# The first expert block's first half and the lists that lead to it, moved ahead of parts of attention unit 10

## The chip, the cores and the metric

The kernel runs on one core of a Trainium2 chip. A time is the device time of one execution in microseconds (us). The core's engines work side by side, each through its own list of instructions in order: TensorE (PE, with its weight loads shown apart as PEld), VectorE (DVE), ScalarE (ACT), GpSimd (POOL) and SyncE (SP), which here issues transfers. An instruction waits for semaphores that others raise, and what stands behind it on its engine waits with it.

## The reference

Attention with random features, then a mixture of eight experts of which each row takes one:

```
proj = einsum('bhsd,md->bhsm', x, omega)             # x: q or k, scaled; 8 batches, 8 heads, 576 rows
phi = exp(h - max(h)) / sqrt(m),  h = proj - sum(x*x)/2
kv = einsum('bhsm,bhsd->bhmd', phi(k), v);  z = sum(phi(k))
attn = (phi(q) @ kv) / (phi(q) . z + 1e-6)           # x of the experts: (4608, 512)
e_idx = argmax(x @ w_gate);  gate_w = softmax(...)[e_idx];  eom = sigmoid(x @ w_output_gate)
out[mask] = gate_w * eom * (relu(x[mask] @ w1[e]) @ w2[e])     # mask: rows with e_idx == e
```

## The kernel before

Rows are cut into four chunks of two batches (1152 rows, nine tiles of 128). A **unit** u is one head of one chunk, 8 per chunk and 32 in all; 128 columns hold its keys' and its queries' features. When a chunk's eight units are done, its rows are sorted into **items**: up to 128 rows of one expert, whose indices are lists that a gather follows. Items run as expert blocks while the next chunks' units go on. So units 8 to 15 run beside the first items.

Every step has a short name; a table `ORDER` (line 70 on) lists all of them, some 3200, in one order, and each engine runs its own steps in that order. A second string, `BANKS`, gives the PSUM bank to each step that opens one, and `FILL` the number of filler products in each of six places. A filler is a product of two constants (512 columns) whose result nobody reads. The names that matter here, for unit u, item n and third g of a unit's nine tiles:

- `ld.t.u`, `ld.v.u`: loads of a unit's turned keys and queries and of its values (SP). `hi.u`, `lo.u`: their fp16 halves, `xhi` on ACT (L588) and `xlo` on POOL (L591).
- `pp.u.g`: projection (PE, L681). `mx.2u.g`, `mx.2u+1.g`: maxima of keys and of queries (DVE, L699). `nb.u.g`: the bias from them (DVE). `ex.2u.g`, `ex.2u+1.g`: exponentials (ACT, L716); they free the bank of `pp`.
- `kv.u`: keys times values (PE, L804); `kvh.u`, `kvs.u`: its halves (ACT, DVE); `kt.u`: these sums turned (PE, L840); `ke.u` (ACT, L849) and `kg.u` (PE, L846): their product with the gates' weights; `gh.u`, `gl.u`: its halves.
- `eh`, `el`, `eT.u`: the queries' halves (ACT, POOL L739) and their transposition by a transfer (SP, L781). `pn.u.0`, `pn.u.5`: numerators of five and four tiles (PE, L867); `xf`: the division (DVE).
- `assign.0`, `places.0`, `lists.0` (DVE), `pid.0` (PE, L1306), `gi.0` (DVE, L1313 and L1339), `controls.0` (DVE): the first chunk's lists of row indices and control words.
- `gx.n`: the gather of an item's rows (POOL, L1584); `<9` ties it behind `eT.9`. `xt.n`: their transposition (SP, L1595).
- `w0h.1.i`, `w0l.1.i`: the halves of the first expert's first weights, which are loaded ahead on the guess that the first item is expert 1's (ACT and DVE, L521 and L526). `sw.0.1`: a branch on ACT and DVE that makes these halves anew if the guess is wrong; it is passed by here.
- `hA.n`, `hB.n`: the two halves of an expert block's first product (PE, L1618); `relu.n`, `rest.n`: halves of its result; `out.n`: the second product (L1651).
- `warm.i`: `FILL[i]` filler products (PE, L479).

`hA.n` waits for `xt.n`, for its bank, and on ACT and DVE for the end of `sw.n.1`, which counts as a writer of the weights' halves whether or not it is passed by:

```
add((name, n), "PE", ..., after=[("xt", n), *cuts_of(n, 1, halves_of[g])] ...
plan.add(("sw", n, w), ("ACT", "DVE"), lambda w=w: switch(w),
         after=[flag_step[n, 1, ("ACT", "DVE")], ("bring", n, w)] + last)
```

Of the kernel before, what the change touches and what calls it, by code (L numbers as in the profile page):

```python
# [113 lines left out]
bounded.0 eh.21 gl.9 xf.8.0 mx.22.0 advance.0:0 ld.t.13 xf.8.5:0 pp.11.1 flag.0.1.ACT+DVE mx.23.0 w0h.2.3 advance.0:1 mx.22.1 pn.9.5 xf.9.5:0 w0h.2.2
advance.0:2 gx.2<9 xt.0 mx.23.1 nb.11.0:0 kv.10.0 el.21 xf.8.5:1 nb.11.1:0 advance.0:3 xf.9.5:1 nb.11.0 w0h.1.3 nb.11.1 advance.0:4 kv.10.1 ex.22.1
ld.t.14 xf.8.5 eT.10 kvh.10 advance.0:5 xf.9.5 w0l.1.3 pn.9.0 kvs.10 xf.9.0:0 w0l.1.2 flag.0.1.SP ex.23.0 pp.11.2 ex.23.1 xf.9.0:1 bring.0.1 ex.22.0
kt.10 advance.0:6 sw.0.1 hi.13.0 pp.12.0 xf.9.0 bring.1.1 advance.0:7 mx.24.0 w0h.2.1 advance.0:8 lo.13.0 warm.3 hA.0 mx.22.2 ke.10 sqr.12 w0h.2.0
mx.25.0 mx.23.2 relu.0.0 advance.0:9 nb.12.0:0 nb.11.2:0 kg.10 advance.0:10 nb.12.0 nb.11.2 ld.v.12 lga.8 w0l.2.1 gx.1<9 hB.0 gh.10 gl.10 rest.0.0
ex.22.2 ex.23.2 w0l.2.2 w0l.2.3 sqa.13 relu.0.1 kv.11.0 ex.24.0 pp.12.1 advance.0 kv.11.1 pp.12.2 w0l.2.0 bring.0.2 sw.0.2 eh.23 mx.24.1 out.0.0
ex.25.0 sw.1.1 el.23 mx.24.2 ld.t.15 xh.8 mx.25.1 nb.12.1:0 ld.n.15 hi.14.0 bring.2.1 kvh.11 pn.10.5 nb.12.1 mx.25.2 ld.n.14 vh.12 ld.v.13 xt.1 eT.11  # L120
rest.0.1 bring.1.2 nb.12.2:0 xl.8 ex.25.1 xf.10.5:0 ex.24.1 nb.12.2 sqr.13 vl.12 out.0.1 pn.10.0 ex.24.2 ex.25.2 xf.10.5:1 sqa.14 xf.10.5 pp.13.0
eh.24 os.0 lo.14.0 kvs.11 sw.1.2 mx.26.0 hA.1 eh.25 kt.11 mx.27.0 ke.11 pp.13.1 ld.v.14 xf.10.0:0 xf.10.0:1 nb.13.0:0 relu.1.0 hB.1 el.24 sqr.14
xf.10.0 kg.11 nb.13.0 xh.9 mx.26.1 ex.26.0 rest.1.0 ld.n.16 mx.27.1 kv.12.0 nb.13.1:0 el.25 nb.13.1 ex.27.0 sw.2.1 sqa.15 pp.13.2 ld.t.16 mx.26.2
ex.27.1 mx.27.2 nb.13.2:0 out.1.0 gh.11 xt.2 eT.12 ex.26.1 relu.1.1 vh.13 gl.11 nb.13.2 pp.14.0 ld.n.17 bring.2.2 ex.27.2 rest.1.1 ex.26.2 sqr.15
mx.28.0 kv.12.1 sqa.16 kvh.12 eh.26 mx.29.0 hi.15.0 lga.9 kvs.12 pn.11.0 pp.14.1 mx.28.1 out.1.1 nb.14.0:0 eh.27 nb.14.0 gx.3<11 xl.9 vl.13 mx.29.1
nb.14.1:0 ex.28.0 put.0<11 bring.3.1 kt.12 el.26 xf.11.0:0 os.1 hA.2 xh.10 rows.4 sqr.16 ex.29.0 nb.14.1 pn.11.5 ex.29.1 xt.3 pp.14.2 ex.28.1 kv.13.0
xf.11.5:0 sw.2.2 ke.12 mx.28.2 lga.10 xf.11.0:1 xf.11.5:1 kg.12 hi.16.0 hB.2 xf.11.5 mx.29.2 gh.12 sw.3.1 nb.14.2:0 gl.12 lo.15.0 nb.14.2 relu.2.0
ld.v.15 ex.28.2 ld.n.18 pn.12.5 ex.29.2 rest.2.0 kv.13.1 relu.2.1 ld.t.17 vh.14 kvh.13 pn.12.0 pp.15.0 el.27 eh.28 kvs.13 eT.13 kt.13 sqa.17 vh.15
xl.10 hA.3 xf.12.5:0 gx.4<12 mx.30.0 ke.13 mx.31.0 kg.13 vl.14 xf.11.0 sqr.17 gh.13 xf.12.0:0 xf.12.0:1 xf.12.5:1 gl.13 xh.11 eh.29 xf.12.0 out.2.0
# [1660 lines left out]
```

## Time and profile before

| | |
|---|---|
| median of 3 runs | 623.45 us (618.49, 623.45, 624.92) |
| the profiled execution | 623.36 us, its span 621.6 us |
| busy in the span | PE 587.6, PEld 451.1, DVE 408.0, ACT 413.9, POOL 361.2 us |
| granted PE clock, mean | 0.996 |

The profiled execution's time is 1.8 us longer than its span, which runs from its first to its last instruction. PE is the engine with the most work; over the span it idles 34 us, and where it does, another engine or a transfer is late.

### The profile page before, as it was taken

Reading aid. Unit: us, or ns where it says so; the run is one execution under the profiler, and the core shown is the slowest. Engines: PE = TensorE matmul, PEld = TensorE weight load, DVE = VectorE, ACT = ScalarE, POOL = GpSimd, SP = SyncE. Lnnn points to the kernel's source line nnn. Section 1 sums busy time; section 2 is a strip of 40 time slices with the busy share of each in tenths; the row PEclk is TensorE's granted clock in tenths of the full one; section 3 lists DMA queues with packets and bytes.
Section 4 is the critical chain, followed back from the end, with each engine's and each line's share of the span. In section 5 each row is a group of like instructions: output and inputs, shape, how many; then the busy total and the mean of one; then the engine's idle time right before and its main releaser. Section 6 shows DMA issues by size and latency. Waiting matters only on the chain. (4 is left out here: it accounts for less than half of the span.)

```text
span 621.6 us, 21399 instructions
## 1 busy us (share of the span) xinstructions
PE 587.6 (95%) x8442; PEld 451.1 (73%) x8442; DVE 408.0 (66%) x1114; ACT 413.9 (67%) x971; POOL 361.2 (58%) x265
## 2 busy tenths in 40 slices
...
GB/s 296 274 291 293 314 269 195 246 268 246 346 208 247 213 215 263 194 197 245 285 236 247 145 203 204 150 227 221 184 147 338 93 91 132 295 65 91 109 289 33
DMA packets 144686, 133.74 MB, mean 215 GB/s; under 512 B 104606, under 2 KB 124448, under 8 KB 143264
## 3 DMA queue, kind: packets, MB, share of 16 engines
...
## 5 line engine op out<-in xcount | busy, mean ns | idle before, releaser
L716 ACT ACTIVATE ef<-pp,nb 128x128 f32<-128x128 f32 x576 | 164.6, 393 | 40.2 <-DVE nb L710 29.6
L699 DVE TENSOR_REDUCE pp<-pp 128x3 f32<-128x384 f32 x192 | 106.7, 562 | 46.6 <-PE pp L681 40.6
L739 POOL TENSOR_TENSOR es<-ef,es 128x1152 f16<-128x1152 f32 x44 | 104.5, 2378 | 38.4 <-ACT es L737 21.7
L1618 PE MATMUL ph<-xt,w1h 128*128 128x128 f16 (+1 forms) x2048 | 122.2, 217 | 1.0 <-issue 0.6
L1618 PEld LDWEIGHTS <-w1h 128*128 128x128 f16 x2048 | 113.5, 98 | 6.9 <-issue 1.7
L1584 POOL DMA_INDIRECT gx<-rows,gi x38 | 41.0, 1079 | 130.1 <-ACTq L1551 63.3
L1629 DVE SCALAR_TENSOR_TENSOR hl<-ph,hh 128x512 f16<-128x512 f32 (+1 forms) x76 | 50.6, 666 | 99.7 <-ACTq L1551 73.8
L1651 PEld LDWEIGHTS <-hh 128*128 128x128 f16 x560 | 51.5, 98 | 54.5 <-issue 0.8
L1625 ACT ACTIVATE hh<-ph 128x512 f16<-128x512 f32 (+1 forms) x76 | 44.7, 591 | 65.6 <-PE ph L1618 50.9
L1618 PE MATMUL ph<-xt,w1l 128*128 128x128 f16 (+1 forms) x1024 | 66.7, 218 | 2.3 <-issue 2.3
L591 POOL TENSOR_TENSOR xlo<-xt,xhi 128x1152 f16<-128x1152 f32 x24 | 57.2, 2381 | 11.2 <-ACT xhi L588 11.1
L1651 PE MATMUL po<-w2h,hh 128*128 128x512 f16 x240 | 62.6, 383 | 0.0
L1651 PE MATMUL po<-w2h,hl 128*128 128x512 f16 x240 | 62.3, 382 | 0.0
L1651 PE MATMUL po<-w2l,hh 128*128 128x512 f16 x240 | 61.6, 379 | 0.0
L1694 ACT ACTIVATE os<-po,gx 128x512 f32<-128x512 f32 (+1 forms) x35 | 24.2, 692 | 54.9 <-PE po L1651 45.6
L1618 PEld LDWEIGHTS <-w1l 128*128 128x128 f16 x1024 | 58.5, 98 | 2.8 <-issue 2.8
L737 ACT CAST es<-ef 128x1152 f16<-128x1152 f32 x44 | 51.6, 1178 | 4.4 <-DMA et<-es 3.5
L1651 PEld LDWEIGHTS <-hl 128*128 128x128 f16 x280 | 27.5, 99 | 33.9 <-issue 1.1
L907 POOL TENSOR_TENSOR xs<-xf,xs 128x576 f16<-128x576 f32 x32 | 40.9, 1281 | 17.4 <-DVE nb L710 6.6
L867 PE MATMUL pn<-kvs,et 128*128 128x81 f16 x768 | 39.9, 201 | 3.1 <-DMA et<-es 1.2
L867 PEld LDWEIGHTS <-et 128*128 128x128 f16 x768 | 34.3, 97 | 8.7 <-issue 3.1
L681 PEld LDWEIGHTS <-xhi 64*128 64x128 f16 x864 | 25.6, 94 | 15.7 <-issue 9.0
(210 smaller groups left out, 1047.9 us busy)
## 6 DMA issues: line engine op xcount, KB each, us to landing
...
xn<-kqn SPq DMA_DIRECT2D x31, 576.0 KB
xt<-kqt SPq DMA_DIRECT2D x31, 576.0 KB
rawv<-v SPq DMA_DIRECT2D x32, 325.0 KB
rows<-xs SPq DMA_DIRECT2D x16, 576.0 KB
...
```

The lines of the kernel that those rows point to most:

```text
L591: plan.add(("lo", u, x), ("POOL",), lambda t0=t0, t1=t1: nc.gpsimd.tensor_tensor(out=xl(u)[:, t0:t1], in0=xt32(u)[:, t0:t1], in1=xh(u)[:, ...
L699: nc.vector.tensor_reduce(out=spare(g, 0)[:, i], in_=banks["pp", 2 * u + i, g][:, 0:3, :], op=ALU.min, axis=AX.X)
L716: nc.scalar.activation(ef(2 * u + i)[:, c, :], banks["pp", 2 * u + i, g][:, c % 3, :], AF.Exp, bias=nb(u)[:, i, c : c + 1], scale=-SK)
L737: nc.scalar.copy(es(slot_es(n))[:, 0], ef(n))
L739: nc.gpsimd.tensor_tensor(out=es(slot_es(n))[:, 1], in0=ef(n), in1=es(slot_es(n))[:, 0], op=ALU.subtract)
L867: nc.tensor.matmul(pn[:, c - c0, :], a[:, c, :], w[:, :, 0 if c < 4 else 1], start=(i == 0 and c == c0), stop=(c == NC - 1 and i == len(op ...
L907: nc.gpsimd.tensor_tensor(out=x[:, :, P + o : P + o + D], in0=xf(u)[:, :, 0:D], in1=x[:, :, o : o + D], op=ALU.subtract)
L1584: return nc.gpsimd.indirect_dma_start(out=gx(n), out_offset=None, in_=rows[0 : (j + 1) * NC * P], in_offset=bass.IndirectOffsetOnAxis(ap=t ...
L1618: nc.tensor.matmul(ph[:, f4, 0:w_], w[qd][:, kk, fo : fo + P], xt(n)[:, x, 0:w_], start=(z == 0 and f4 == 0 and x == 0), stop=(z == 1 and ...
L1625: nc.scalar.activation(hh(n)[:, sl, 0:w_], banks["ph", n, g][:, :, 0:w_], AF.Relu)
L1629: nc.vector.scalar_tensor_tensor(out=hl(n)[:, sl, 0:w_], in0=banks["ph", n, g][:, :, 0:w_], scalar=0.0, in1=hh(n)[:, sl, 0:w_], op0=ALU.ma ...
L1651: nc.tensor.matmul(po, x(n)[:, f, :], w[f // 2][:, f % 2, :], start=(f == 0 and a == 0), stop=(f == FC - 1 and a == 2))
```

## The change

Only the three tables change; every step and its computation stay, but for four filler products.

```
@@ ORDER, around unit 10 (two lines of each kernel)
-assign.0:3 places.0:1 warm.1 kg.8 pp.10.2 assign.0:4 hi.12.0 ex.21.0 kvs.9 lo.11.0 assign.0:5 kt.9 mx.20.2 gh.8 assign.0:6 w0h.1.2 places.0 assign.0
-eT.9 mx.21.2 controls.0:0 lists.0:0 ke.9 nb.10.2:0 gl.8 controls.0:1 lists.0:1 controls.0:2 warm.2 pn.8.0 nb.10.2 sqa.12 lists.0 warm.5 pid.0 w0l.1.1
...
+assign.0:3 places.0:1 warm.1 kg.8 pp.10.2 assign.0:4 hi.12.0 ex.21.0 kvs.9 lo.11.0 assign.0:5 kt.9 gh.8 assign.0:6 w0h.1.2 places.0 assign.0 eT.9
+lists.0:0 ke.9 lists.0:1 warm.2 sqa.12 lists.0 pid.0 mx.20.2 gi.0:0 gi.0 gx.0<9 lo.12.0 mx.21.2 nb.10.2:0 gl.8 pn.8.0 warm.5 controls.0:0 nb.10.2
...
-FILL = (5, 6, 8, 4, 4, 3,)
+FILL = (5, 6, 7, 1, 4, 3,)
```

The moves, in full: `lists.0`, `pid.0`, `gi.0` and `gx.0` go ahead of `mx.21.2`, `nb.10.2`, `gl.8`, `pn.8.0`, `controls.0` and `w0l.1.1`, and `lists.0` ahead of `mx.20.2` too; `lo.12.0` goes behind `gx.0`. `ld.v.11` and `ld.t.13` go behind `xt.0`. `w0h.1.3` goes ahead of `w0h.2.3` and `w0h.2.2`; `ex.22.0` goes ahead of `ex.22.1`, `ex.21.1` ahead of `ex.21.2`. `sw.0.1` and `hA.0` go ahead of `kt.10` and `pp.12.0`. `warm.3` goes from the place right ahead of `hA.0` to one between `kv.10` and `pn.9.0`, and has one product in place of four; `warm.2` has seven in place of eight. `BANKS` follows: the filler left in `warm.3` takes the bank that `ex.22.0` leaves, and `hA.0` takes it after that. From `hB.0` on the two orders are the same.

On DVE the difference at the lists reads as follows; `pp_2` is the bank of unit 10's last third, `rt`, `r_eq`, `r_itc`, `pid` and `gi` are the lists':

```order
-L699 TENSOR_REDUCE pp_2_1802<-pp_2_1802 128x3
 L1157 COPY r_exs<-rt_1605 128x9
 L1079 TENSOR_TENSOR place<-cmt,rt_1605 128x1152
 L1160 TENSOR_TENSOR rt_1605<-rt_1605,cft 128x8
+L1172 COPY rt_1605<-cft 128x18
+L1175 TENSOR_TENSOR r_eq<-keys,rt_1605 128x9x8
+L1183 TENSOR_TENSOR r_itc<-r_eq,rt_1605 128x18x8
+L699 TENSOR_REDUCE pp_2_1802<-pp_2_1802 128x3
+L1313 TENSOR_REDUCE pid_1860<-pid_1860 128x8
+L1339 CAST gi_1872<-pid_1860 128x8
 L699 TENSOR_REDUCE pp_2_1802<-pp_2_1803 128x3
```

The first maximum now stands between the lists and their cast to indices, and the second behind that cast.

On SP, around the first gather's transposition, before (`et_1842` is `eT.9`, `rawv_1962` `ld.v.11`, `xt_1978` `ld.t.13`, `xt_2044` `xt.0`) and then now (`xt_2040` is `xt.0`, `rawv_2042` `ld.v.11`, and `xt_2044` is `ld.t.13`):

```order
L781 DMA_TRANSPOSE et_1842<-es_1749 128x18x128
L660 DMA rawv_1952<-v 128x650
L660 DMA rawv_1962<-v 128x650
L658 DMA xt_1978<-kqt 128x1152
L1595 DMA_TRANSPOSE xt_2044<-gx_1968 128x8x128
L658 DMA xt_2073<-kqt 128x1152
```

```order
L781 DMA_TRANSPOSE et_1841<-es_1749 128x18x128
L660 DMA rawv_1955<-v 128x650
L1595 DMA_TRANSPOSE xt_2040<-gx_1874 128x8x128
L660 DMA rawv_2042<-v 128x650
L658 DMA xt_2044<-kqt 128x1152
L658 DMA xt_2075<-kqt 128x1152
```

The transposition, which waits for the gather, went ahead of two loads.

On PE, from the end of `pp.11.2` (`pp_2_2127`) to the start of `hA.0` (`ph_0`), before and then now; `kv_2049<-cmt` is `kt.10`, `pp_0` is `pp.12.0`, `fill` is `warm.3`:

```order
L681 MATMUL pp_2_2127<-omh,xlo_1830 128x128
L840 LDWEIGHTS kvs_2078
L840 MATMUL kv_2049<-cmt,kvs_2078 128x128
...
L681 LDWEIGHTS xhi_1823
L681 MATMUL pp_0_2179<-omh,xhi_1823 128x128
...
L479 MATMUL fill_2219<-omh 128x512
L1618 LDWEIGHTS w1h_85
L1618 MATMUL ph_0_2224<-xt_2044,w1h_85 128x128
```

```order
L681 MATMUL pp_2_2131<-omh,xlo_1830 128x128
...
L1618 LDWEIGHTS w1h_85
L1618 MATMUL ph_0_2175<-xt_2040,w1h_85 128x128
...
L840 LDWEIGHTS kvs_2080
L840 MATMUL kv_2049<-cmt,kvs_2080 128x128
...
L681 LDWEIGHTS xhi_1823
L681 MATMUL pp_0_2229<-omh,xhi_1823 128x128
```

`hA.0` now follows `pp.11.2` directly, and what stood between them follows `hA.0`; the fillers between them are gone. The steps ahead of `sw.0.1` on ACT are the same ones in both kernels; `ex.22.0`, which stood last of them, is now the first exponential of unit 11.

## Rows read from the trace of the kernel before

**Rows 1.** Page, busy time, share of the span and instructions of each engine

```profile
PE 587.6 (95%) x8442; PEld 451.1 (73%) x8442; DVE 408.0 (66%) x1114; ACT 413.9 (67%) x971; POOL 361.2 (58%) x265
```

**Rows 2.** Stretches: length, busy PE, PEld, DVE, ACT, POOL, clock, DMA share, GB/s

```profile
96.00:112.00 16.00, 13.92 (x209) 10.22 (x208) 15.64 (x57) 15.80 (x39) 9.25 (x6) 1.00 1.02 210
104.00:112.00 8.00, 6.97 (x106) 5.74 (x105) 7.86 (x29) 7.80 (x20) 4.16 (x3) 1.00 1.07 186
112.00:144.00 32.00, 32.00 (x484) 24.67 (x482) 27.27 (x65) 29.97 (x69) 22.62 (x17) 1.00 1.04 262
```

**Rows 3.** Timeline of PE (start us, us, engine line op tiles, idle before)

```profile
106.24 0.61 PE L867 MATMUL pn<-kvs,et 128*128 128x81 f16 x12 [0.26 <-DVE xf L885]
...
107.37 0.33 PE L681 MATMUL pp<-omh,xlo 64*128 64x128 f16 x6
...
108.30 0.27 PE L840 MATMUL kv<-cmt,kvs 128*128 128x128 f16 x2 [0.60 <-DVE den L881]
...
108.91 0.36 PE L681 MATMUL pp<-omh,xlo 64*128 64x128 f16 x6
...
109.39 1.02 PE L479 MATMUL fill<-omh 128*128 128x512 f16 x4
...
110.47 1.95 PE L1618 MATMUL ph<-xt,w1h 128*128 128x128 f16 x32
...
113.23 1.95 PE L1618 MATMUL ph<-xt,w1h 128*128 128x128 f16 x32
```

**Rows 4.** A stretch for line 479 alone, the fillers: length, busy PE, PEld, clock

```profile
95.50:112.00 16.50, 3.73 (x15) 1.33 (x15) 1.00 1.01 206
```

**Rows 5.** Timeline of DVE

```profile
95.64 0.56 DVE L699 TENSOR_REDUCE pp<-pp 128x3 f32<-128x384 f32 x1
...
99.18 1.23 DVE L526 SCALAR_TENSOR_TENSOR w1l<-r,w1h 128x1024 f16<-128x1024 f32 x1
...
100.78 0.15 DVE L1339 CAST gi<-pid 128x8 uint32<-128x8 f32 x1
...
108.22 1.21 DVE L526 SCALAR_TENSOR_TENSOR w1l<-r,w1h 128x1024 f16<-128x1024 f32 x1
```

**Rows 6.** Timeline of POOL

```profile
96.75 2.37 POOL L591 TENSOR_TENSOR xlo<-xt,xhi 128x1152 f16<-128x1152 f32 x1 [0.50 <-ACT xhi L588]
...
101.23 2.03 POOL L1584 DMA_INDIRECT gx<-rows,gi  x1 [2.10 <-DVE den L883]
```

**Rows 7.** Timeline of SP's queue

```profile
94.63 3.23 SPq L781 DMA_TRANSPOSE et<-es  x1
...
99.05 0.38 SPq L658 DMA_DIRECT2D xt<-kqt  x1
...
105.60 1.26 SPq L1595 DMA_TRANSPOSE xt<-gx  x1
```

**Rows 8.** Timeline of ACT

```profile
105.86 0.99 ACT L716 ACTIVATE ef<-pp,nb 128x128 f32<-128x128 f32 x3
...
106.77 2.57 ACT L716 ACTIVATE ef<-pp,nb 128x128 f32<-128x128 f32 x9
...
109.54 1.15 ACT L588 CAST xhi<-xt 128x1152 f16<-128x1152 f32 x1 [0.20 <-ACTq L1546]
...
111.56 0.35 ACT L849 CAST kvf<-kv 128x256 f16<-128x256 f32 x1
```

**Rows 9.** Page, transfers by line, with their size

```profile
xt<-kqt SPq DMA_DIRECT2D x31, 576.0 KB
rawv<-v SPq DMA_DIRECT2D x32, 325.0 KB
```

**Rows 10.** Timeline of PE at two later waits, and a stretch around the second

```profile
350.04 0.32 PE L681 MATMUL pp<-omh,xhi 64*128 64x128 f16 x5 [1.45 <-ACT ef L716]
...
479.18 0.80 PE L1618 MATMUL ph<-xt,w1l 128*128 128x128 f16 x8 [1.06 <-issue]
...
478.00:482.80 4.80, 3.73 (x19) 1.79 (x17) 1.32 (x4) 2.27 (x3) 0.33 (x1) 0.65 0.99 288
```

More of the change, by code (lines that the diff above doesn't have):

```diff
@@ L110 @@
 kt.8 weigh.0:1 nb.10.0 assign.0:0 nb.10.1:0 weigh.0:2 w0h.1.1 ex.20.0 assign.0:1 kvh.9 weigh.0 nb.10.1 assign.0:2 ke.8 ex.20.1 places.0:0 scales.0
-assign.0:3 places.0:1 warm.1 kg.8 pp.10.2 assign.0:4 hi.12.0 ex.21.0 kvs.9 lo.11.0 assign.0:5 kt.9 mx.20.2 gh.8 assign.0:6 w0h.1.2 places.0 assign.0
-eT.9 mx.21.2 controls.0:0 lists.0:0 ke.9 nb.10.2:0 gl.8 controls.0:1 lists.0:1 controls.0:2 warm.2 pn.8.0 nb.10.2 sqa.12 lists.0 warm.5 pid.0 w0l.1.1
-pn.8.5 kg.9 ex.21.2 ex.21.1 gi.0:0 pp.11.0 lo.12.0 controls.0:3 ld.v.10 xf.8.0:0 gi.0 ex.20.2 ld.v.11 controls.0 xf.8.0:1 w0l.1.0 gh.9 gx.0<9
@@ L114 @@
[L114 to L129, printed above, removed]
@@ L130 @@
-bring.4.1 xf.12.5 rest.2.1 pp.15.1 nb.15.0:0 lo.16.0 el.28 sqa.18 kv.14.0 mx.30.1 bring.3.2 vl.15 out.2.1 nb.15.0 xt.4 mx.31.1 ex.30.0 nb.15.1:0
-sw.3.2 xl.11 el.29 bring.4.2 sqr.18 pn.13.0 nb.15.1 ex.31.0 ex.31.1 relu.3.0 rest.3.0 ld.v.16 put.1<12 pp.15.2 lga.11 ld.n.19 kv.14.1 xh.12 hi.17.0
-mx.30.2 hB.3 mx.31.2 xf.13.0:0 nb.15.2:0 nb.15.2 xf.13.0:1 kvh.14 eT.14 xl.12 ex.30.1 kvs.14 ex.31.2 xf.13.0 relu.3.1 pn.13.5 xf.13.5:0 lga.12
+assign.0:3 places.0:1 warm.1 kg.8 pp.10.2 assign.0:4 hi.12.0 ex.21.0 kvs.9 lo.11.0 assign.0:5 kt.9 gh.8 assign.0:6 w0h.1.2 places.0 assign.0 eT.9
@@ new lines @@
+lists.0:0 ke.9 lists.0:1 warm.2 sqa.12 lists.0 pid.0 mx.20.2 gi.0:0 gi.0 gx.0<9 lo.12.0 mx.21.2 nb.10.2:0 gl.8 pn.8.0 warm.5 controls.0:0 nb.10.2
+controls.0:1 controls.0:2 controls.0:3 w0l.1.1 pn.8.5 kg.9 ex.21.1 ex.21.2 pp.11.0 ld.v.10 xf.8.0:0 ex.20.2 controls.0 xf.8.0:1 w0l.1.0 gh.9 bounded.0
+eh.21 gl.9 xf.8.0 mx.22.0 advance.0:0 xf.8.5:0 pp.11.1 flag.0.1.ACT+DVE mx.23.0 w0h.1.3 w0h.2.3 advance.0:1 mx.22.1 pn.9.5 xf.9.5:0 w0h.2.2
+advance.0:2 gx.2<9 xt.0 ld.v.11 ld.t.13 mx.23.1 nb.11.0:0 kv.10.0 el.21 xf.8.5:1 nb.11.1:0 advance.0:3 xf.9.5:1 nb.11.0 nb.11.1 advance.0:4 kv.10.1
@@ new lines @@
+ex.22.0 ex.22.1 ld.t.14 xf.8.5 eT.10 kvh.10 advance.0:5 xf.9.5 w0l.1.3 warm.3 pn.9.0 kvs.10 xf.9.0:0 w0l.1.2 flag.0.1.SP ex.23.0 pp.11.2 ex.23.1
+xf.9.0:1 bring.0.1 sw.0.1 hA.0 kt.10 advance.0:6 hi.13.0 pp.12.0 xf.9.0 bring.1.1 advance.0:7 mx.24.0 w0h.2.1 advance.0:8 lo.13.0 mx.22.2 ke.10 sqr.12
+w0h.2.0 mx.25.0 mx.23.2 relu.0.0 advance.0:9 nb.12.0:0 nb.11.2:0 kg.10 advance.0:10 nb.12.0 nb.11.2 ld.v.12 lga.8 w0l.2.1 gx.1<9 hB.0 gh.10 gl.10
+rest.0.0 ex.22.2 ex.23.2 w0l.2.2 w0l.2.3 sqa.13 relu.0.1 kv.11.0 ex.24.0 pp.12.1 advance.0 kv.11.1 pp.12.2 w0l.2.0 bring.0.2 sw.0.2 eh.23 mx.24.1
```

15 lines of the change are left out of this document (14 added, 1 removed).

## The prediction

> **What bounds the kernel now.** I read the page's busy times first, then equal stretches, then the engines' timelines around the change. TensorE (PE) is busy 95% of the span [rows 1]: whatever delays PE delays the end, and whatever only delays another engine does so when PE runs out of work. The stretches show two states [rows 2]. From 96 to 112 us PE is busy 13.92 of 16 us, while VectorE (DVE) has 15.64 and ScalarE (ACT) 15.80: here those two set the pace and PE waits for them. From 112 to 144 us PE has 32.00 of 32: it is the bound, and a delay or gain it enters with is carried on. So the question is when PE gets into that full stretch. I take as mark the start of hB.0, the second half of the first expert block, at 113.23 [rows 3]: everything from there on stands in the same order in both kernels.
>
> A ceiling comes out of the same rows. Between 96 and 112 us PE idles 16 - 13.92 = 2.08 us, and 3.73 us of its busy time are filler products [rows 2, 4]. If the change removed all of that, it would bring 5.8 us, 0.93% of 623.36 us, the profiled execution's time. So no saving here can pass 1%, which is about what a measurement of this kernel can tell from no change.
>
> **The lists.** On DVE the two maxima of unit 10's last third (0.56 us each, in a stream about 0.46) and w0l.1.1 (1.2 us) stood ahead of the list's cast gi.0; now one maximum stands between lists and gi.0, and that one covers PE's sum pid.0. gi.0 ended at 100.78 + 0.15 = 100.93 [rows 5]. Ahead of it go 0.46 + 1.2 and, of the two maxima, what pid.0 does not take up anyway, about 0.4: some 2.1 us, so it ends near 98.8. Nothing is saved on DVE by that: the same instructions run ahead of w0l.1.2 in both orders, DVE is full, and the list's links now follow each other at once and can stall 0 to 0.3 us.
>
> **The gather and the two queues it is moved past.** gx.0 began at 101.23, 0.3 us behind gi.0 [rows 6]. It is also tied to eT.9, the transposition, whose entry on SP's queue ends at 94.63 + 3.23 = 97.86 and whose data must land later, at the latest at 101.1, since at 101.23 the wait was put down to DVE [rows 6, 7]. So the gather starts between 98.9 and 101.1; I take 100, the middle, a gain of 1.2 us. On GpSimd lo.12.0, which ran from 96.75, now waits behind it, until the gather's 2.03 us are over near 102 [rows 6]; its 2.37 us then end near 104.4, and its only reader in this stretch, pp.12.0, ran at 108.5. That costs nothing.
>
> SP issued the transposition xt.0 at 105.60, 4.37 us behind the gather's start [rows 6, 7]; the same distance gives 104.4 (103.3 to 105.5). xt.0 was not what hA.0 waited for last, so this gains nothing by itself. But ld.v.11 and ld.t.13, the latter issued at 99.05, now stand behind the wait for the gather: with xt.0's 1.26 us and ld.v.11's issue ld.t.13 comes at about 106.2. It feeds hi.13.0, which ACT reached at 109.54 [rows 8]. The two loads hold 325 and 576 KB [rows 9], 0.92 MB; at the 186 GB/s that the stretch from 104 to 112 us moved [rows 2] that is an estimate of 4.9 us from 105.7, so ld.t.13 lands near 110.6 (109.5 to 111.7). ACT then waits 1.1 us (0 to 2.2) at hi.13.0, and relu.0.0 and ke.10 stand behind it. In the trace hi.13.0's start to ke.10's end took 111.91 - 109.54 = 2.37 us [rows 8], so ke.10 ends at 113.0 (111.9 to 114.1). kg.10, one step ahead of hB.0 on PE, waits for ke.10.
>
> **PE.** Two edits meet here. The fillers: warm.2 has one product less and warm.3 three less, four at 1.02 / 4 = 0.25 us each [rows 3]. Those of warm.2 stand where PE waits anyway. Those of warm.3 stood right ahead of hA.0 and ended at 110.41; hA.0 began at 110.47. What hA.0 can start from otherwise: its bank is the one that ex.22.0 leaves, ACT's exponentials end at 106.77 + 2.57 = 109.34, and ACT is past sw.0.1, the branch on the first weights, at 109.54 [rows 8]; DVE's w0l.1.2 ends at 108.22 + 1.21 = 109.43 [rows 5]. So without the fillers hA.0 could have begun near 109.6. These gates do not move: the same exponentials, only in another order, and the same halves of weights stand ahead of sw.0.1 on both engines, and both are full. I take 109.8 for the stalls above (109.6 to 110.1).
>
> The order: kt.10 and pp.12.0, from 108.30 to 108.91 + 0.36 = 109.27 [rows 3], lay in PE's wait and cost nothing. Now they stand behind hA.0, in PE's full stretch, and cost their length: 0.97 us with the pipeline's end, about 0.85 in a stream. What PE has in their place is idle time: pp.11.2 ended at 107.70 [rows 3]. It will end later, since the one filler left now stands ahead of pn.9.0 in the bank that ex.22.0 has to leave, and ex.22.0 is now ACT's first of that unit, at about 105.9 to 106.7: pn.9.0 goes from 106.24 to about 106.9. That is inside the wait too, if hA.0 really starts at 109.8.
>
> **The sum.** hA.0 to the start of hB.0 took 113.23 - 110.47 = 2.76 us, kg.10 among it. Now 109.8 + 2.76 + 0.85 = 113.41, against 113.23: +0.2 us. kg.10 would be free at about 113.1 (112.0 to 114.2) and reached at 113.33, so ke.10 mostly hides behind pp.12.0; for its upper half I add 0.1. Forecast: +0.3 us, 623.36 + 0.3 = 623.7 us. Bounds: with hA.0 at 109.6 and 0.8 for the two it is 0.0; with ke.10 at 114.1 it is 114.3 - 113.23 = +1.1. The profiled execution lies 0.1 us below the median of the three runs, 623.45, which scatter from 618.49 to 624.92; that scatter is larger than any term here.
>
> **Rivals.** *Faster: hA.0 follows pp.11.2 at once.* That is what the smaller fillers look made for. If ACT and DVE came to sw.0.1 some 2 us earlier, hB.0 would start at 107.7 + 2.76 + 0.85 = 111.3, 1.9 us earlier: 621.4. For it speaks that PE idles 2.08 us here; against it that ACT is busy 15.80 of 16 us and nothing is taken off it ahead of the branch.
>
> *Slower: PE's clock falls in the new wait.* Between pp.11.2 and hA.0 PE now stands still for 1.5 to 2 us without fillers, after another 0.7 ahead of the one filler. In this trace the granted clock fell once in the middle of the work: PE idled 1.06 us until 479.18, and the clock averages 0.65 from 478 to 482.8 [rows 10]. That is 4.8 x 0.35 = 1.7 us of PE's work lost, at 1.2 in place of 2.4 GHz for 3.4 us. Against it: at 350.04 an idle time of 1.45 us had no such end, and the clock stayed at 1.00 from 96 to 112 us [rows 2, 10]. It decides from the point at which hA.0 starts at the lower level: 623.7 + 1.7 = 625.4. The Trainium skill bears on it: "TensorE: Matmul & The Clock Gate", Part 1, says that half rate is the default and only recent activity holds the full rate, so fillers that are taken out of a wait are no pure gain. By that rule the time would be this rival's; the fall at 479 agrees with it, the stretch at 350 shows that one gap does not always do it.
>
> *Slower: ld.t.13 comes later than estimated.* Each microsecond beyond 111.7 goes to hi.13.0, ke.10 and kg.10 in full; two more give 623.7 + 0.8 + 2 = 626.5.
>
> *The change does not do what it says.* If eT.9 lands at 101, the gather starts as before and xt.0 lands as before or later; PE's part stays as summed, with hA.0 at 110.1 or so: +0.5, 623.9, hard to tell from the forecast.
>
> **How the numbers follow.** Forecast and the case in which the gather stays, 0.62; the clock 0.20; the faster case 0.10; the late load 0.08. The likeliest gives 623.7. The range goes down to the faster case less the scatter of the runs, 621.4 - 2, and up to the late load's 626.5: 619.5 to 626.5. None of these cases leaves the band of 1% (617.2 to 629.6), so what I give to both sides is what I have not seen in the 480 us behind this stretch, where a shifted start meets branches and transfers anew: 0.05 faster, 0.07 slower, 0.88 the same.
>
> **What would show it.** In the profile after: gx.0 on GpSimd near 100 with lo.12.0 behind it; pn.9.0 near 106.9 behind one filler; idle time on PE of over 1 us ahead of hA.0, ended by ACT, with hA.0 at 109.6 to 110.1; kt.10 and pp.12.0 behind it and hB.0 at 113.2 to 114.3; hi.13.0 at 110 to 111.7, held by a transfer. I am wrong in the mechanism if hA.0 starts ahead of 109.0 (ACT was freer than it looks), if PE's clock reads below 1.00 between 106 and 116 us, or if hB.0 lies outside 113.0 to 114.5; and in the result if the two kernels differ by more than 3 us while hB.0 does not, since the difference then arises behind the change.

## The result, and the profile after

The changed kernel took 629.6 us, median of six runs (625.81 to 634.28), against 622.34 for the kernel before (six runs, 618.49 to 625.94): ratio 1.0123, 95% interval 1.0078 to 1.0168. It is 1.2% slower, outside the range of the prediction. The profiled execution took 632.93 us, its span 631.1.

The page's busy line [rows 1] and the stretches [rows 2] of the changed kernel:

```profile
PE 588.8 (93%) x8438; PEld 453.6 (72%) x8438; DVE 411.8 (65%) x1114; ACT 414.6 (66%) x971; POOL 362.4 (57%) x265
```

```profile
96.00:112.00 16.00, 10.41 (x131) 8.07 (x126) 15.33 (x49) 12.63 (x30) 9.23 (x5) 0.83 0.77 190
104.00:112.00 8.00, 4.79 (x42) 4.59 (x42) 8.00 (x29) 4.90 (x10) 5.14 (x3) 0.66 0.79 222
112.00:144.00 32.00, 28.97 (x454) 23.65 (x453) 24.04 (x57) 26.16 (x65) 17.79 (x12) 0.98 0.81 203
```

PE's work is the same; it idles 3.5 us more from 96 to 112, 3 us more from 112 to 144, and the granted clock is 0.66 from 104 to 112, in part 1.2 in place of 2.4 GHz. ACT, which was full, works 3.2 us less in the first stretch: ACT and PE wait for a third engine. DVE is as busy as before, and is the suspect for that reason: busy need not be work.

GpSimd's timeline [rows 6]:

```profile
100.99 1.18 POOL L1584 DMA_INDIRECT gx<-rows,gi  x1 [3.88 <-DVE pp L699]
102.20 2.39 POOL L591 TENSOR_TENSOR xlo<-xt,xhi 128x1152 f16<-128x1152 f32 x1
```

DVE's timeline [rows 5], with two later rows:

```profile
100.19 0.17 DVE L1339 CAST gi<-pid 128x8 uint32<-128x8 f32 x1
...
100.95 0.19 DVE L855 SCALAR_TENSOR_TENSOR kvs<-kv,kvs 128x32 f16<-128x32 f32 x1
...
101.53 4.15 DVE L526 SCALAR_TENSOR_TENSOR w1l<-r,w1h 128x1024 f16<-128x1024 f32 x1
...
105.68 0.14 DVE L1225 TENSOR_TENSOR ctl<-r_sw,rt 128x8 int32<-128x8 f32 x1
...
105.89 1.19 DVE L526 SCALAR_TENSOR_TENSOR w1l<-r,w1h 128x1024 f16<-128x1024 f32 x1
107.00 0.16 DVE L1345 TENSOR_TENSOR oi<-pid,r_none 128x8 uint32<-128x8 f32 x1
...
119.29 0.57 DVE L699 TENSOR_REDUCE pp<-pp 128x3 f32<-128x384 f32 x1 [2.35 <-PE pp L681]
...
122.84 0.22 DVE L710 SCALAR_TENSOR_TENSOR nb<-pp,sqs 128x6 f32<-128x6 f32 x2
```

PE's timeline [rows 3]:

```profile
99.13 0.39 PE L1306 MATMUL pid<-r_itc,place 128*128 128x16 f16 x9 [0.91 <-DVE r_itc L1183]
...
101.19 0.31 PE L867 MATMUL pn<-kvs,et 128*128 128x81 f16 x4 [1.34 <-DVE kvs L855]
...
107.21 0.48 PE L681 MATMUL pp<-omh,xhi 64*128 64x128 f16 x5 [3.29 <-DVE oi L1345]
...
109.05 4.59 PE L804 MATMUL kv<-rawv,ef 128*128 128x130 f32 x20
113.49 0.38 PE L479 MATMUL fill<-omh 128*128 128x512 f16 x1
113.70 0.61 PE L867 MATMUL pn<-kvs,et 128*128 128x81 f16 x12
...
115.61 1.96 PE L1618 MATMUL ph<-xt,w1h 128*128 128x128 f16 x32 [0.44 <-ACTq L1546]
...
119.21 1.95 PE L1618 MATMUL ph<-xt,w1h 128*128 128x128 f16 x32
...
124.36 0.83 PE L804 MATMUL kv<-rawv,ef 128*128 128x130 f32 x5 [2.31 <-DVE kvs L855]
```

ACT's timeline [rows 8]:

```profile
107.23 1.06 ACT L521 ACTIVATE w1h<-r 128x1024 f16<-128x1024 f32 x1 [2.70 <-DVE oi L1345]
...
115.71 1.15 ACT L588 CAST xhi<-xt 128x1152 f16<-128x1152 f32 x1 [0.20 <-ACTq L1546]
...
123.09 1.66 ACT L716 ACTIVATE ef<-pp,nb 128x128 f32<-128x128 f32 x6 [2.55 <-DVE nb L710]
```

Three places stand out. `gl.8` (L855) comes at 100.95, and PE waits 1.34 us for it in `pn.8.0`. `w0l.1.1`, the product of two SBUF operands that took 1.23 us before, takes 4.15 us while `lo.12.0` runs on GpSimd; behind it stand the control words that ACT loads (L1225) and `oi` (L1345), which frees the bank in which `pp.11.1` goes on. PE waits 3.29 us, ACT 2.70. And at 119.29 DVE has waited 2.35 us for `pp.12.0`, after which `nb.11.2`, ACT's `ex.22.2` and PE's `kv.11` are late in turn: 2.31 us on PE behind `hB.0`. Smaller than these three is a wait of 0.91 us on PE ahead of `pid.0`, for the last link of the lists; in the kernel before PE came to `pid.0` without one.

This execution had one more difference, before the change's place: in `pp` and `pn` of unit 8 the granted clock was 0.57 from 72 to 76 us, 1.00 before, and everything after lies 0.85 us later (`kvh.9` starts at 94.99, before at 94.14). So the table below counts from the start of `kvh.9` in the same trace.

### The profile page after: what moved, and what is told of

It is laid out like the page before. It is cut to its first block, busy times and chain, and to the rows that moved or that the text cites. A ratio compares the mean times of both kernels' runs of the same rounds, so it can differ in the third digit from the quotient of the medians.

```text
span 631.1 us, 21392 instructions
## 1 busy us (share of the span) xinstructions
PE 588.8 (93%) x8438; PEld 453.6 (72%) x8438; DVE 411.8 (65%) x1114; ACT 414.6 (66%) x971; POOL 362.4 (57%) x265
## 3 DMA queue, kind: packets, MB, share of 16 engines
q8 instruction: 82, 1.34, 0.9%
## 5 line engine op out<-in xcount | busy, mean ns | idle before, releaser
L739 POOL TENSOR_TENSOR es<-ef,es 128x1152 f16<-128x1152 f32 x44 | 104.9, 2388 | 45.1 <-ACT es L737 25.8
L1629 DVE SCALAR_TENSOR_TENSOR hl<-ph,hh 128x512 f16<-128x512 f32 (+1 forms) x76 | 50.5, 665 | 97.4 <-ACTq L1551 74.5
L591 POOL TENSOR_TENSOR xlo<-xt,xhi 128x1152 f16<-128x1152 f32 x24 | 57.1, 2381 | 15.5 <-ACT xhi L588 15.3
```

What stands on the lines that cost most here:

```text
L591: plan.add(("lo", u, x), ("POOL",), lambda t0=t0, t1=t1: nc.gpsimd.tensor_tensor(out=xl(u)[:, t0:t1], in0=xt32(u)[:, t0:t1], in1=xh(u)[:, ...
L739: nc.gpsimd.tensor_tensor(out=es(slot_es(n))[:, 1], in0=ef(n), in1=es(slot_es(n))[:, 0], op=ALU.subtract)
L1629: nc.vector.scalar_tensor_tensor(out=hl(n)[:, sl, 0:w_], in0=banks["ph", n, g][:, :, 0:w_], scalar=0.0, in1=hh(n)[:, sl, 0:w_], op0=ALU.ma ...
```

## The experiments

The theory at the start: all of the loss follows from the collision of `lo.12.0` with `w0l.1.1`. The rivals: TensorE's clock, and the order itself (`hA.0` ahead of `pp.12.0`, or the lists). The last two columns, each from the one profiled execution of its run, are how much later than before `kvh.10` (L820) and the first `hl` (L1629, the low half of `hA.0`'s result) start, counted from `kvh.9`; before, these are 106.61 - 94.14 = 12.47 and 115.24 - 94.14 = 21.10 us. The first four experiments ran on one chip (before: 617.09 us), the next four on a second (622.91), the last four on a third (622.97). Where an edit moves a step that opens a bank, `BANKS` follows it.

| run | ratio, 95% interval | `w0l.1.1`, `w0l.1.0`, us | `kvh.10` | `hl` |
|---|---|---|---|---|
| the changed kernel | 1.0123 [1.0078, 1.0168] | 4.15, 1.19 | +6.2 | +8.1 |
| e1_lo_first | 1.0087 [1.0052, 1.0121] | 1.22, 1.18 | +2.7 | +4.6 |
| e2_hA_alone | 1.0068 [1.0034, 1.0102] | 1.22, 1.19 | +0.7 | +2.8 |
| e3_w0l_late | 1.0102 [1.0051, 1.0153] | 3.32, 1.21 | +5.6 | +8.6 |
| e4_fillers_in_wait | 1.0123 [1.0075, 1.0170] | 4.15, 1.18 | +4.7 | +6.6 |
| e5_hA_maxima | 0.9988 [0.9964, 1.0012] | 1.22, 1.19 | +0.7 | +0.7 |
| e6_lists_alone | 1.0010 [0.9986, 1.0034] | 1.22, 1.19 | +2.0 | +1.1 |
| e7_lo_in_six | 1.0069 [1.0044, 1.0093] | 1.45, 1.27 | +2.8 | +4.7 |
| e8_mended | 1.0030 [1.0003, 1.0057] | 1.22, 1.18 | +1.3 | +1.2 |
| e9_fillers_alone | 0.9977 [0.9951, 1.0004] | 1.22, 1.18 | 0.0 | 0.0 |
| e10_mended_collision | 1.0056 [1.0028, 1.0084] | 1.22, 3.10 | +3.6 | +3.7 |
| e11_after_again | 1.0109 [1.0062, 1.0156] | 4.17, 1.18 | +5.0 | +6.9 |
| e12_parts_joined | 0.9991 [0.9964, 1.0017] | 1.22, 1.22 | +1.4 | +0.5 |

**e1, `lo.12.0` back ahead of the gather.**

```
-gi.0 gx.0<9 lo.12.0 mx.21.2
+gi.0 lo.12.0 gx.0<9 mx.21.2
```

> The changed kernel with one step moved back: lo.12.0, the low part that GpSimd works out, runs ahead of the first gather again. Theory: in the changed kernel lo.12.0 (102.20 to 104.59) and w0l.1.1 on DVE (101.53, 4.15 us in place of 1.23) keep each other out, the sums of which PE and ACT wait for stand behind w0l.1.1, and all of the loss follows from that. Then w0l.1.1 is back at 1.2 to 1.3 us, PE's wait of 3.29 us ahead of pp.11.1 is under 1 us, the granted clock stays at 1.00 from 106 to 113, hB.0 starts at 113 to 114, and the time is 621.5 to 624.5, a ratio to the kernel before of 0.998 to 1.004. Rival of the clock (fewer fillers let TensorE's clock fall): nothing changes, 628 to 631, ratio 1.010 or more. Rival of the order (hA.0 ahead of kt.10 and pp.12.0, or the list's links in one row, cost the time): 627 to 630, ratio 1.007 or more.

`w0l.1.1` is back at 1.22 us and the wait ahead of `pp.11.1` is gone, but the ratio is 1.0087, not 1.004 or less. The collision is real and the theory that it is all falls. On ACT `hi.13.0` now waits for its load, which the change put behind `xt.0`:

```profile
112.12 1.15 ACT L588 CAST xhi<-xt 128x1152 f16<-128x1152 f32 x1 [1.46 <-DMA xt<-kqt]
```

**e2, the second half of the change alone, on the kernel before.**

```
-ex.22.1 ... pn.9.0 ... ex.22.0 kt.10 advance.0:6 sw.0.1 hi.13.0 pp.12.0 ... lo.13.0 warm.3 hA.0
+ex.22.0 ex.22.1 ... warm.3 pn.9.0 ... sw.0.1 hA.0 kt.10 advance.0:6 hi.13.0 pp.12.0 ... lo.13.0
-FILL = (5, 6, 8, 4, 4, 3,)
+FILL = (5, 6, 7, 1, 4, 3,)
```

> The kernel before with the second half of the change alone: the filler product ahead of pn.9.0, sw.0.1 and hA.0 ahead of kt.10 and pp.12.0, ex.22.0 ahead of ex.22.1, and the smaller counts of fillers. Lists, gather and lo.12.0 stand as before. Theory: no collision on DVE, so w0l.1.1 takes 1.2 us and the time moves by no more than the prediction's sum, -1 to +1.5 us, ratio 0.998 to 1.003. Rival of the clock: with four fillers gone the granted clock falls below 1.00 between 104 and 114 us, hB.0 starts 1.5 to 5 us later than 113.23, 625 to 629, ratio 1.004 to 1.011. Rival of the order (the later kt.10 delays ke.10, and PE waits 2.3 us near 124 as in the changed kernel): 625 to 630, ratio 1.004 or more, with the clock at 1.00.

1.0068 at a granted clock of 1.00 from 96 to 128 us: the rival of the order. DVE's row and four of PE's:

```profile
112.93 0.57 DVE L699 TENSOR_REDUCE pp<-pp 128x3 f32<-128x384 f32 x1 [2.67 <-PE pp L681]
```

```profile
106.92 0.62 PE L867 MATMUL pn<-kvs,et 128*128 128x81 f16 x12
...
109.25 1.96 PE L1618 MATMUL ph<-xt,w1h 128*128 128x128 f16 x32 [0.85 <-ACTq L1546]
...
112.85 1.95 PE L1618 MATMUL ph<-xt,w1h 128*128 128x128 f16 x32
...
118.00 1.39 PE L804 MATMUL kv<-rawv,ef 128*128 128x130 f32 x10 [2.31 <-DVE kvs L855]
```

`hA.0` is early and `hB.0` too, by 0.2 us (`kvh.9` starts at 93.96 here), as the prediction's sum had it within 0.4. The loss comes behind the mark: DVE stands at `mx.24.0`, the first maximum of the now later `pp.12.0`, and in its queue behind that wait the maxima of `pp.11.2`, which PE had finished at 108.4 (108.07 + 0.33). PE pays at `kv.11`.

**e3, DVE's two products moved behind `mx.22.1` in the changed kernel.**

```
-controls.0:3 w0l.1.1 pn.8.5 ... xf.8.0:1 w0l.1.0 gh.9 ... mx.22.1 pn.9.5
+controls.0:3 pn.8.5 ... xf.8.0:1 gh.9 ... mx.22.1 w0l.1.1 w0l.1.0 pn.9.5
```

> The changed kernel with DVE's two halves of weights, w0l.1.1 and w0l.1.0, moved behind mx.22.1, that is behind the control words, the sums oi and xf.8.0; lo.12.0 stays behind the gather. Theory: lo.12.0 is over, or nearly, when DVE comes to w0l.1.1, and nothing that ACT or PE waits for stands right behind it: the two take 1.2 us each (up to 2 for the first), oi is written near 102.5, PE's wait ahead of pp.11.1 is under 1.2 us and the time 621.5 to 625, ratio 0.998 to 1.005. Rival of the clock, of the list's links and of hA.0's place: unchanged at 628 to 631. Rival that lo.12.0 is slow or late for its own reader, pp.12.0: unchanged too.

A miss that shows the mechanism. `lo.12.0` is over, but the next product of GpSimd, `el.21` (L739), has just begun; GpSimd's row, then DVE's:

```profile
105.03 2.39 POOL L739 TENSOR_TENSOR es<-ef,es 128x1152 f16<-128x1152 f32 x1
```

```profile
105.19 3.32 DVE L526 SCALAR_TENSOR_TENSOR w1l<-r,w1h 128x1024 f16<-128x1024 f32 x1
```

`w0l.1.1` ends at 108.51, 1.09 us behind `el.21`'s end at 107.42: it had waited it out.

**e4, thirteen filler products in PE's wait in the changed kernel.**

```
-xf.8.5:0 pp.11.1 ... w0l.1.3 warm.3 pn.9.0
+xf.8.5:0 warm.3 pp.11.1 ... w0l.1.3 pn.9.0
-FILL = (5, 6, 7, 1, 4, 3,)
+FILL = (5, 6, 7, 13, 4, 3,)
```

> The changed kernel with the filler of warm.3 taken from ahead of pn.9.0 and thirteen products of it put ahead of pp.11.1, where PE waits 3.29 us (13 x 0.25 us is about that long). The collision stays. Theory: the wait stays and w0l.1.1 still takes about 4 us, but PE is not idle and the granted clock stays at 1.00, so kv.10 takes 2.5 us in place of 4.6; of the 8 us lost about 3 come back, 625.5 to 628. Rival of the clock (the collision alone is hidden, the half clock is the loss): 622 to 624.5, ratio 1.004 or less. If the clock's fall were only a companion, with PE waiting for ACT and DVE anyway: 628.5 to 631.

The stretch from 104 to 112, in the columns of the stretches above, then PE's and DVE's timelines with the fillers, `pp.11.1`, `kv.10` and `oi`:

```profile
104.00:112.00 8.00, 7.77 (x99) 5.68 (x97) 8.00 (x32) 6.07 (x15) 4.12 (x2) 1.00 0.91 253
```

```profile
103.85 2.98 PE L479 MATMUL fill<-omh 128*128 128x512 f16 x13
106.88 0.34 PE L681 MATMUL pp<-omh,xhi 64*128 64x128 f16 x6
...
107.97 2.47 PE L804 MATMUL kv<-rawv,ef 128*128 128x130 f32 x20
```

```profile
105.81 0.16 DVE L1345 TENSOR_TENSOR oi<-pid,r_none 128x8 uint32<-128x8 f32 x1
```

In this stretch the clock stays at 1.00 (from 96 to 104 us it is 0.79, as in e11), and `kv.10` takes 2.47 us in place of 4.59, yet the ratio is 1.0123 as without the fillers. Against e11, the changed kernel with the same clock up to 104 us, `hl` gains 0.3 us. The fillers outran the wait, though: `oi` was done at 105.97 and `pp.11.1` began 0.9 us later, where in e11 it went on 0.05 us behind `oi`. So 0.3 us is the least that the fall of the clock cost in that stretch, and an estimate of the most is 0.3 + 0.9 = 1.2 us, of 6.9.

**e5, e2 with the maxima of `pp.11.2` ahead of `mx.24.0`.**

```
-advance.0:7 mx.24.0 w0h.2.1 advance.0:8 lo.13.0 mx.22.2 ke.10 sqr.12 ... mx.23.2 ... nb.11.2:0 ... nb.11.2
+advance.0:7 mx.22.2 mx.23.2 nb.11.2:0 nb.11.2 sqr.12 mx.24.0 w0h.2.1 advance.0:8 lo.13.0 ke.10 ...
```

> The second half of the change alone, as in the run before of that name, with one thing more: DVE's maxima and sums of pp.11.2 (mx.22.2, mx.23.2, nb.11.2) and sqr.12 stand ahead of mx.24.0, which waits for the later pp.12.0. Theory of the head of the queue: in that run hB.0 was early (112.85), but DVE stood 2.67 us at mx.24.0 with the maxima of pp.11.2 behind it, so ACT's ex.22.2 and PE's kv.11 came 2.6 us late; now PE's wait ahead of kv.11 (2.31 us) falls under 0.4 us, hh's low part L1629 starts near 115 and not at 117.85, and the time is that of the kernel before, ratio 0.996 to 1.002. Rival of ke.10 (kv.11 is held by the later kt.10 and kg.10, whose bank it needs, not by the maxima): the wait stays at 2 us and more, ratio 1.005 to 1.009. Rival of the clock: the fillers taken out still cost, ratio 1.003 or more with a granted clock under 1.00 between 104 and 114.

The maxima on DVE and `kv.11` on PE:

```profile
109.74 1.23 DVE L699 TENSOR_REDUCE pp<-pp 128x3 f32<-128x384 f32 x2
```

```profile
115.48 1.39 PE L804 MATMUL kv<-rawv,ef 128*128 128x130 f32 x10 [0.23 <-DVE kvs L855]
```

As the theory had it: the wait goes from 2.31 to 0.23 us, `hl` from +2.8 to +0.7, the ratio from 1.0068 to 0.9988. The queue's head on DVE was most of what this half cost, 2.1 of 2.8 us at `hl`; `kt.10` and `ke.10`, as late as in e2, were not. The total is no longer told from no change.

**e6, the first half of the change alone, without its collision** (e1, with `kt.10`, `pp.12.0`, the fillers and `hA.0` as before).

```
-warm.3 pn.9.0 ... sw.0.1 hA.0 kt.10 advance.0:6 hi.13.0 pp.12.0 ... lo.13.0
+pn.9.0 ... kt.10 advance.0:6 sw.0.1 hi.13.0 pp.12.0 ... lo.13.0 warm.3 hA.0
```

> The first half of the change alone and without its collision: the lists' links in one row ahead of unit 10's maxima, the gather after them, but lo.12.0 ahead of the gather as in the kernel before, and kt.10, pp.12.0, the filler of four products and hA.0 in the order of before. Theory: no wait ahead of kv.11 (under 0.4 us), no 4 us product on DVE; what is left is gl.8, which now stands behind the sum pid.0 and two maxima, so PE waits 1.3 us ahead of pn.8.0's last products, the granted clock averages about 0.8 from 96 to 104, kvh.10 comes about 2 us late and hB.0 about 2 us, ratio 1.001 to 1.006. Rival: the list's order costs nothing by itself (the prediction's sum), hB.0 within 0.5 us, ratio 0.998 to 1.001.

```profile
100.25 0.31 PE L867 MATMUL pn<-kvs,et 128*128 128x81 f16 x4 [1.35 <-DVE kvs L855]
```

The wait for `gl.8` is there in PE's row above, and `kvh.10` is 2.0 us late; the clock stayed at 1.00, so that part of the expectation failed, and with the late `hl` at only +1.1 the total is no longer told from no change.

**e7, `lo.12.0` in six instructions in the changed kernel** (the product, L591, is L595 here; lines behind it are three higher).

```
+n = 6 if u == 12 else 1
+w = (t1 - t0) // n
+for a in range(t0, t1, w):
+    nc.gpsimd.tensor_tensor(out=xl(u)[:, a : a + w], ...)
```

> The changed kernel with lo.12.0 as six instructions of 192 columns in place of one of 1152, on GpSimd at the same place. Theory of exclusion by instruction (whoever started holds the other off until its instruction ends): w0l.1.1 gets in between two pieces, starts behind at most one piece (0.4 to 0.6 us) and takes 1.3 to 1.9 us, lo.12.0's later pieces are held in turn; kvh.10 comes about 3 us earlier than in the changed kernel, ratio 1.007 to 1.010, about that of the run with lo.12.0 ahead. Rival of shared speed (both run at once, each slowed): w0l.1.1 still takes 3 us or more, ratio 1.011 to 1.014. Rival of priority (DVE yields to GpSimd at every piece until the last): 4 us as before.

The first piece on GpSimd and `w0l.1.1` on DVE:

```profile
102.11 1.18 POOL L595 TENSOR_TENSOR xlo<-xt,xhi 128x192 f16<-128x192 f32 x1
```

```profile
101.43 1.45 DVE L526 SCALAR_TENSOR_TENSOR w1l<-r,w1h 128x1024 f16<-128x1024 f32 x1
```

Same start, same partner, and 1.45 us in place of 4.15: what keeps the two apart goes by the instruction. Now GpSimd waits (1.18 us for a piece, 0.54 for a piece that meets no such product).

**e8, the three causes mended in the changed kernel.**

```
-lists.0 pid.0 mx.20.2 gi.0:0 gi.0 gx.0<9 lo.12.0 mx.21.2 nb.10.2:0 gl.8 pn.8.0
+lists.0 gl.8 pid.0 mx.20.2 gi.0:0 gi.0 lo.12.0 gx.0<9 mx.21.2 nb.10.2:0 pn.8.0
```

To this comes the move of the maxima on DVE from e5.

> The changed kernel with three steps moved: lo.12.0 back ahead of the gather, gl.8 ahead of the sum pid.0, and mx.22.2, mx.23.2, nb.11.2 and sqr.12 ahead of mx.24.0. Theory: the three losses (the collision, gl.8 behind the lists, the maxima behind mx.24.0) are gone one by one: w0l.1.1 at 1.2 us, no wait over 0.6 us at pn.8.0, under 0.4 us at kv.11; hB.0 within 1 us of the kernel before, ratio 0.996 to 1.002. If something else of the change costs time (the fillers, xt.0's place on SP's queue, ld.v.11 and ld.t.13 behind it): 1.004 or more.

The waits for `gl.8` and ahead of `kv.11` are gone, the one for `oi` is down to 0.70 us, and 1.2 us are left at `hl`, ratio 1.0030. A part of the rest stands on ACT and then on PE:

```profile
111.52 1.15 ACT L588 CAST xhi<-xt 128x1152 f16<-128x1152 f32 x1 [1.94 <-DMA xt<-kqt]
```

```profile
113.94 0.19 PE L846 MATMUL kv<-wgh,kvf 128*128 128x32 f16 x1 [0.69 <-ACT kvf L849]
```

This is `ld.t.13` behind `xt.0`, `hi.13.0` waiting for it and `kg.10` for `ke.10`, a term of the prediction that in the changed kernel itself the other delays hide (`hi.13.0` waits 0.20 us there, and not for the load).

**e9, the kernel before with the smaller counts of fillers alone** (the line `FILL` of e2).

> The kernel before with the smaller counts of fillers alone: seven products in place of eight in warm.2, one in place of four in warm.3, which stays at its old place right ahead of hA.0, behind kt.10 and pp.12.0. Theory: hA.0 was held by the three products and starts some 0.8 us earlier (109.6 in place of 110.47, counted from a common start), hB.0 likewise, the granted clock stays at 1.00 from 104 to 114, and the time is 0.2 to 0.9 us shorter, ratio 0.997 to 1.000. Rival of the clock: it falls in the wait that is left ahead of hA.0, hB.0 is 1 us or more late, ratio 1.002 to 1.006.

PE's `hA.0` and `hB.0`, and ACT:

```profile
109.82 1.95 PE L1618 MATMUL ph<-xt,w1h 128*128 128x128 f16 x32
...
112.58 1.95 PE L1618 MATMUL ph<-xt,w1h 128*128 128x128 f16 x32
```

```profile
114.13 1.14 ACT L716 ACTIVATE ef<-pp,nb 128x128 f32<-128x128 f32 x4 [0.67 <-DVE nb L710]
```

Both halves start 0.65 us earlier at a clock of 1.00; by `hl` it is given back, since ACT then waits 0.67 us for `nb.11.2`, whose time DVE sets. The interval, 0.9951 to 1.0004, allows a gain and doesn't show one.

**e10, e8 with the collision put back.**

```
-gi.0 lo.12.0 gx.0<9 mx.21.2
+gi.0 gx.0<9 lo.12.0 mx.21.2
```

> The kernel with the mended order of the run before, with the collision put back: gl.8 ahead of pid.0 and the maxima of pp.11.2 ahead of mx.24.0, but lo.12.0 behind the first gather as in the changed kernel. Against the mended kernel this differs by one step on GpSimd's queue. Theory: w0l.1.1 takes 3.5 to 4.2 us, oi and the control words come 3 us later, PE waits over 2 us ahead of pp.11.1, kvh.10 is 2.5 to 4 us later than in the mended kernel, and the ratio to the kernel before is 1.005 to 1.010. Rival: the collision is taken up by waits that are there anyway, kvh.10 within 1 us of the mended kernel, ratio 1.001 to 1.005.

GpSimd, DVE and PE:

```profile
102.04 2.39 POOL L591 TENSOR_TENSOR xlo<-xt,xhi 128x1152 f16<-128x1152 f32 x1
```

```profile
100.98 1.22 DVE L526 SCALAR_TENSOR_TENSOR w1l<-r,w1h 128x1024 f16<-128x1024 f32 x1
...
102.41 3.10 DVE L526 SCALAR_TENSOR_TENSOR w1l<-r,w1h 128x1024 f16<-128x1024 f32 x1
105.43 0.15 DVE L1345 TENSOR_TENSOR oi<-pid,r_none 128x8 uint32<-128x8 f32 x1
```

```profile
105.64 0.32 PE L681 MATMUL pp<-omh,xhi 64*128 64x128 f16 x5 [2.62 <-DVE oi L1345]
```

Here `w0l.1.1` gets through ahead of `lo.12.0` and `w0l.1.0` is held: it ends 1.08 us behind `lo.12.0`'s end at 104.43. Against e8 one step on one queue is moved, and `kvh.10` is 2.3 us and `hl` 2.5 us later. The intervals of the two ratios overlap, so this price is shown at the two marks of one execution each, and not in the total by itself.

**e11, the changed kernel again, and e12, what the runs point to, joined** (e8's lists; `kt.10` and `pp.12.0` ahead of `hA.0`, `ld.v.11` and `ld.t.13` ahead of `xt.0` as before; one filler ahead of `hA.0`).

```
-pid.0 ... gx.0<9 lo.12.0 ... gl.8 ... ld.v.10 ... xt.0 ld.v.11 ld.t.13 ... sw.0.1 hA.0 kt.10 ... pp.12.0
+gl.8 pid.0 ... lo.12.0 gx.0<9 ... ld.v.10 ld.v.11 ld.t.13 ... xt.0 ... kt.10 ... sw.0.1 ... pp.12.0 ... warm.3 hA.0
```

> The changed kernel once more, on the chip on which the mended kernels run, so that the parts can be summed on one chip. Expected by its first measurement: ratio 1.009 to 1.016, w0l.1.1 at 4.15 us, waits of 3.3 us ahead of pp.11.1 and of 2.3 us ahead of kv.11. If the collision, gl.8 and the maxima are the whole, its kvh.10 is 5.5 to 6.5 us later than in the kernel before and hh's low part L1629 7.5 to 9 us.

> What the runs point to, joined: the lists and the gather ahead as in the changed kernel, with lo.12.0 ahead of the gather, gl.8 ahead of pid.0, and ld.v.11 and ld.t.13 ahead of xt.0 on SP's queue as in the kernel before; kt.10 and pp.12.0 ahead of hA.0 as in the kernel before, and the one filler product right ahead of hA.0. Theory: w0l.1.1 at 1.2 us, no wait over 0.6 us at pn.8.0, none at kv.11, hi.13.0 not held by its load (in the mended kernel it waited 1.94 us for it); hB.0 between 1 us earlier and 0.5 us later than in the kernel before, ratio 0.996 to 1.001. If the lists' new order costs time in itself: hB.0 over 1 us late, 1.002 or more.

e11 repeats the result without the half-clock stretch at 72 us: `hl` +6.9, a little less than expected. The parts come to nearly that: the lists 1.1 (e6), the second half 2.8 (e2), the collision 2.3 (e11 less e1) to 2.5 (e10 less e8), together 6.2 to 6.4. Some 0.6 us are not given to one step. The later load is the candidate, since `hi.13.0` waits 1.46 us for it in e1 and 0.43 in e6; no run takes it alone. e12 is level with the kernel before, 0.9991. No version beats the kernel before by more than its interval.

## Why the prediction was wrong

**`lo.12.0` behind the gather: "That costs nothing."** This is the first step that failed, with 2.3 to 2.5 us: a term put at nothing. I looked for the cost of a moved step only at its reader. What it costs lies at an instruction that shares no data with it: while GpSimd's product of SBUF operands runs, DVE's product of two SBUF operands stands still, and counts as busy. In the kernel before `lo.12.0` ended at 99.12 [rows 6], and `w0l.1.1` began at 99.18 [rows 5]. The trace of before held a warning, GpSimd's row and DVE's:

```profile
104.53 2.40 POOL L739 TENSOR_TENSOR es<-ef,es 128x1152 f16<-128x1152 f32 x1
```

```profile
106.57 1.46 DVE L526 SCALAR_TENSOR_TENSOR w1l<-r,w1h 128x1024 f16<-128x1024 f32 x1
```

The product ends at 108.03, 1.10 us behind `el.21`'s end at 106.93, and so takes 0.25 us more than the 1.21 of its neighbour [rows 5]. The Trainium skill, "SBUF — State Buffer", section "SBUF: two separate sides", says that DVE and GpSimd share a pair of ports as an exclusive lock, which a DVE operation with two SBUF inputs wants against a GpSimd operation that reads SBUF, and that the other one blocks fully. By that rule the move would have been priced, as an estimate, at about GpSimd's 2.4 us; the trace agrees (4.15, 3.32 and 3.10 us in place of 1.22), and e7 shows that the lock goes by the instruction.

**The mark.** That "everything from there on stands in the same order in both kernels" is true of PE's list, and the sum for it was good: in e2, which has no collision, `hB.0` starts 18.89 us behind `kvh.9`, 19.09 before [rows 3]: 0.2 us earlier, where +0.2 was forecast. In the changed kernel it is 119.21 - 94.99 = 24.22, outside the bounds that the prediction set for it. But that `kt.10` and `pp.12.0` "cost their length" left out DVE: the maxima of `pp.12.0` stand there ahead of those of `pp.11.2`. That is the second failed step, worth 2.1 us of the 2.8 (e2 less e5). A product that is moved behind another takes its reader with it, and all that is queued behind that reader.

**The lists.** That the list's "links now follow each other at once and can stall 0 to 0.3 us" counted the links and not the bystander: `gl.8`, now behind them, keeps PE waiting 1.34 us. With the rest of the lists this is the 1.1 us of e6. The lists also took longer than summed: PE waits 0.91 us ahead of `pid.0` for the last link, and `gi.0` ended 100.36 - 94.99 = 5.37 us behind `kvh.9`, 99.5 in the time of before, where 98.8 was forecast. In e8 and e12, which mend `gl.8`, this wait on PE is still there (0.91 and 0.90 us), and `kvh.10` is 1.3 and 1.4 us late; that the one makes the other is not shown.

**The clock.** The rival with a chance of 0.20 said that it would fall in the wait between `pp.11.2` and `hA.0`, for want of fillers. It did fall, but around the 3.29 us ahead of `pp.11.1`, a wait that the rival did not have; in e2 and e9, where the fillers are taken out and the collision is not there, it stays at 1.00 from 96 to 128 us. That the sign came true is luck. Its price from 104 to 112 us was 0.3 to 1.2 us by e4, where the rival had 1.7.

**The later load.** 1.94 us at `hi.13.0` in e8 and 1.46 in e1, within the 0 to 2.2 forecast, above its 1.1. It is hidden in the changed kernel by the larger delays.

**The rest.** Counted from `kvh.9`, `gx.0` began 6.00 us behind it, 7.09 before: a gain of 1.1, forecast 1.2. That is luck in part: 1.2 was the middle of two bounds, and `gi.0`, from which one of them was worked out, came 0.7 us later than forecast. `pn.9.0` behind its one filler came at 12.96 in e2, where 106.9 - 94.14 = 12.8 was forecast; `hA.0` at 15.29 there, forecast 109.8 - 94.14 = 15.7. So the terms on PE were right, and the time was lost where no term stood. The ceiling of 5.8 us bounded the gain (its fillers were counted from 95.50 us on and its idle time from 96, so it is up to 0.3 us too high); no such bound was drawn for the loss.
